# Scores of the first batch by pairs of heads, in two half-size PSUM areas, with a new step list

## The chip, the cores and the metric

One core of a Trainium2 chip runs the kernel. The core has five engines with queues of their own: TensorE (PE, matrix products; PEld is its loading of the stationary operand), VectorE (DVE), ScalarE (ACT), GpSimd (POOL) and SyncE (SP, which here only starts transfers). They wait for each other by semaphores. TensorE writes only to PSUM, which has eight banks of 512 fp32 columns on 128 partitions; ACT and DVE read it. Transfers (DMA) between main memory and the on-chip SBUF are started from the queues of SP, ACT and POOL and run beside the engines. The metric is the device time of one execution in microseconds (us), the median over several runs.

## The reference

The kernel computes attention with a forgetting gate for 8 batches of 8 heads, 576 positions and 64 features, and then a two-layer network on the result. Inputs and output are float32.

```python
scores = scale * np.matmul(q, k.transpose(0, 1, 3, 2))       # 8 x 8 x 576 x 576
cum = np.cumsum(np.log(np.clip(f, 0.0001, 1.0)), axis=-1)
scores = np.where(causal, -1e9, scores + cum[:, :, :, None] - cum[:, :, None, :])
attn = np.exp(scores - max); attn = attn / (sum(attn) + 1e-09)
x = np.matmul(attn, v)                                        # to 4608 x 512
h = x @ w_in                                                  # 512 x 2048
out = (h * sigmoid(h)) @ w_out                                # 2048 x 512
```

The part of the decay that depends on the query falls out of the quotient, so the kernel multiplies the values, and the ones of the denominator, by `exp(-cum)` of their key, and leaves the scores themselves alone.

## The kernel before

**Units of work.** A unit `n` is a batch and half its heads: `n = 2 * batch + group`, 16 units of four heads. Of each unit, q and k are loaded as four transfers each (L120), a strip of 32 partitions per head; they are cast to bf16 (L136 on POOL; one cast, the keys of n=0, on ACT, L134) and transposed in blocks of 32 by DVE (L279). After that a head's 64 features lie as two halves of 32 in its strip of 32 partitions. A score is therefore two matmuls of 32 rows each, accumulated (L350), with `tile_position` at the strip of the head. Keys stand on the PSUM partitions and queries along the columns. Only the key blocks at or below the diagonal are computed: 576 + 448 + 320 + 192 + 64 = 1600 columns a head.

**Scores.** `chunk` (L315) takes a score area `sc` of four banks, one bank of 512 columns per head (`patt`, tag `att`, one buffer), fills it, and has ACT write `exp(scale * sc)` as bf16 to `u` for all four heads in one instruction (L360). For batch 0 (n = 0 and 1) the 1600 columns are laid out so that queries 0 to 255 come first, then 256 to 511, then the rest, and are cut at 384, 832, 1280 and 1600 (`SPLIT_CUTS`, L307): steps `S n.c` (L367). There the causal mask is added by a matmul of an identity with a block of -30000 (`neg`, L338), ahead of the scores that it covers. For the other 14 units the columns of all units form one stream, cut every 512: steps `s0` to `s43` (L371). Their mask is applied to `u` afterwards by POOL (L387, steps `m`).

**Products.** `products` (L399) makes denominators and numerators from `u`: `w_bf` or the weighted values `vp` as stationary operand, four heads side by side on 32 output partitions each (L429). For batch 0 it uses one-bank areas `pn`: steps `f`, `h` (queries 0 to 255), `d`, `n` (256 to 511) and `e` (512 to 575), where f and d make a unit's denominators and h and n its numerators. The f's take log and exp of the denominator on ACT (L450, L451), the d's a reciprocal on DVE (L453). Whole units later use the same four-bank area as the scores (`ps`, steps `D`, `N`, `P`), with reciprocals in quarters (steps `R`, L468). DVE multiplies numerator and reciprocal into `xT` (L457).

**Network.** The first layer makes `hp` of 128 by 512 by four matmuls (L482), ACT takes tanh (L490) and DVE forms `gt` (L493): steps `A`. For the first group of 512 tokens it goes in halves of 256 tokens: 32 steps `H`. Steps `B` are quarters of an output tile of the second layer, four matmuls each (L516); every fourth `B` ends with a copy on ACT (L526) and a store (L527). `w_in` comes in four quarters, steps `I0` to `I3`, two transfers each from POOL's queue (L190); step `H` number 1 to 4 needs I0, 5 to 8 I1, 9 to 12 I2, 13 to 16 I3, and so again for the second 16. `w_out` comes in four steps `O`. Areas `pn`, `wps`, `hp`, `po` and the idle matmul's come from one pool of four one-bank buffers (`pbig`), in turn.

**Order.** Nothing is scheduled by a planner when the kernel is built. The text `ORDER` (L18) is a list of steps, and each engine's queue holds its instructions in the order of that list. Steps `y`, `z` are cast and transpose of the first 256 positions of n = 0 and 1; `G`, `c`, `t` loading, cast and transpose of their rest; `L`, `C`, `T` loading, cast and transpose of a later unit; the digit after the point is 0 for q and 1 for k. `l`, `u`, `w` are the log, the running sum and exp, and the transpose of the decay. `W b.c` loads a chunk of 128 values of a batch, `V b.c` multiplies it by the weights on POOL. `Z1` is one matmul on zeros whose result is not used. `g`, `o` are transfers of one element that wait for a quarter of a weight.

Of the kernel before, what the change touches and what calls it, by code (L numbers as in the profile page):

```python
# [12 lines left out]
P = 128  # L13
# [5 lines left out]
    l y0.0 y0.1 u z0.1 z0.0 w z1.1 y1.0 S0.0 G0.0 G0.1 z1.0 W0.3 V0.0 c0.0 c0.1 S1.0 I0 t0.0  # L19
    W0.2 t0.1 f0 V0.1 G1.1 S0.1 V0.3 I1 f1 G1.0 L2.1 V0.2 h0 c1.0 c1.1 W0.4 h1 L2.0 S0.2 I2  # L20
    d0 H H I3 S0.3 t1.0 t1.1 H C2.1 C2.0 S1.1 L3.0 n0 H H O2 T2.1 S1.2 H H d1 L3.1 H H S1.3
    n1 V0.4 H H H H H H T2.0 H O1 H C3.0 H H O0 L4.1 T3.0 s0 e0 L4.0 H H O3 s1 C3.1 H W1.4 H
    H T3.1 Z1 m2.0 s2 W1.3 H H H W1.0 g1 s3 e1 H m2.3 H s4 H m3.0 W1.1 H m2.1 m2.4 m3.1 m2.2
    H C4.1 B s5 m3.3 W1.2 B T4.1 m3.2 C4.0 B B D2 T4.0 R2.0 V1.4 B B R2.2 R2.3 B V1.3 s6
    V1.0 L5.0 L5.1 B m3.4 V1.1 W2.4 V1.2 C5.0 B C5.1 L6.0 C6.0 W2.2 B R2.1 P3 R3.1 B B W2.3
    R3.2 R3.0 B s7 B L6.1 m4.0 R3.3 B N3 g2 B W2.0 T5.0 T5.1 A g3 s8 A m4.2 L7.0 A A s9 T6.0
    V2.2 m4.1 m4.3 A m4.4 A A m5.0 D4 A A C6.1 V2.0 V2.3 s10 R4.2 L7.1 A A V2.4 T6.1 A m5.1
    s11 A W2.1 A A R4.3 s12 A B m5.3 W3.4 L8.1 B C7.0 m5.4 m6.0 V2.1 C7.1 V3.4 L8.0 R4.1 B
    s13 B B m5.2 m6.1 W3.2 R4.0 T7.0 T7.1 s14 B C8.0 W3.1 B C8.1 L10.1 W3.0 B P5 R5.1 V3.1
    R5.0 B m6.2 L9.1 B B W4.1 R5.3 s15 m6.4 B B T8.1 B o1 m6.3 R5.2 L9.0 V3.0 P6 W4.4 B V3.2  # L30
    T8.0 B m7.0 A A W3.3 s16 A V3.3 A A L10.0 W4.0 A R6.3 s17 A C10.1 A A C9.0 C10.0 A s18
    T9.0 A C9.1 A m8.0 A R6.2 s19 R6.1 A A V4.4 m7.4 A m7.2 B T9.1 m7.3 s20 B m7.1 B R6.0
    m8.2 V4.1 B P7 L12.0 B R7.3 m8.1 B B W5.4 W4.2 s21 m8.4 W5.1 R7.2 R7.0 W4.3 R7.1 L11.0 B
    B m8.3 B L11.1 T10.1 P8 B B A A s22 V4.3 R8.1 m9.0 A A B s23 B V5.4 T10.0 V4.2 A A R8.3
    s24 L12.1 A m9.3 C11.0 A A R8.2 s25 B A C11.1 A W5.2 s26 T11.1 V4.0 A A m9.1 B T11.0 s27
    m9.4 m9.2 m10.3 m10.2 R8.0 A A A B P9 R9.0 W5.3 C12.1 B R9.2 B m10.0 B s28 C12.0 R9.1 B
    B m10.4 m10.1 L13.0 T12.0 R9.3 V5.1 B C13.0 L14.0 L14.1 P10 B A V5.3 A R10.1 B L13.1 B
    W5.0 T12.1 V5.2 s29 A B R10.2 R10.3 B W6.2 A s30 A A m11.1 A m11.0 A C13.1 s31 m11.2 A B
    A m12.0 T13.0 T13.1 s32 V5.0 W6.1 R10.0 B m11.3 B A C14.1 L15.1 m12.1 s33 B A m11.4 A
    P11 A A m12.2 A R11.0 L15.0 R11.1 C15.1 B V6.1 s34 C15.0 W6.0 m12.4 m12.3 B B B R11.3  # L40
    V6.0 R11.2 P12 B A A A T14.1 s35 W6.4 B C14.0 V6.4 B W6.3 m13.0 B B s36 V6.3 W7.1 R12.3
    T14.0 m13.2 R12.2 A A V6.2 A B s37 A A R12.1 B s38 B W7.2 B A m14.0 m13.3 m13.4 s39
# [10 lines left out]
def kernel(  # L53
# [43 lines left out]
    patt = ctx.enter_context(tc.tile_pool(name="patt", bufs=1, space=bass.MemoryType.PSUM))  # L97
    pbig = ctx.enter_context(tc.tile_pool(name="pbig", bufs=4, space=bass.MemoryType.PSUM))

# [215 lines left out]
    def chunk(pieces):  # L315
        sc = patt.tile([P, QH, 512], FP32, name="sc", tag="att")
# [18 lines left out]
        for n, kb, q0, w, o, low in runs:  # L335
            if low:
                for j in range(QH):
                    nc.tensor.matmul(  # L338
                        sc[:, j, o : o + w],
                        lhsT=ident[:, :],  # L340
                        rhs=neg[:, P - w : P],
                        start=first,
                        stop=False,
                    )
                first = False
        for i, (n, kb, q0, w, o, low) in enumerate(runs):
            for x in range(2):
                for j in range(QH):
                    r = slice(j * 32, (j + 1) * 32)
                    nc.tensor.matmul(  # L350
                        sc[:, j, o : o + w],
# [7 lines left out]
        for n, c0, c1 in pieces:  # L359
            nc.scalar.activation(  # L360
                out=us[n][:, :, c0:c1],
                in_=sc[:, :, at : at + c1 - c0],
                func=ACT.Exp,
                scale=scale,
            )
            at += c1 - c0

    def scores(n, c):
        chunk([(n, SPLIT_CUTS[c], SPLIT_CUTS[c + 1])])


    def stream(i):
# [7 lines left out]
        chunk(pieces)  # L380
# [211 lines left out]
    for step in ORDER.split():  # L592
        if step == "H" and gpool is None:
            setup_pool.__exit__(None, None, None)
            gpool = ctx.enter_context(tc.tile_pool(name="gpool", bufs=2))
# [31 lines left out]
```

## Time and profile before

| what | value |
|---|---|
| median of 9 runs | 353.06 us (352.22 to 353.87) |
| the profiled execution | 353.87 us, span 352.1 us |
| PE busy | 327.5 us, 93% of the span |
| DVE, ACT, POOL busy | 223.3, 209.8, 128.9 us |
| moved by DMA | 42.54 MB, mean 121 GB/s |
| the chain that ended last, by engine | PE 79%, DMA 5%, ACT 4%, DVE 4%, SP's queue 3% |

The span goes from the first to the last instruction in the trace; what the run's time has on top lies around it. A line of the chain or of the order in time begins with the start and the duration in us. Then come engine, line of the kernel, operation and tiles, output ahead of the arrow and inputs behind it, with partitions and elements, and how many such instructions (x). The brackets at the end give how long the engine had been idle before, and whose end released it. In the tables of stretches, each stretch has its length, then for each engine the busy time and the number of instructions, then the granted PE clock, the mean busy share of the DMA engines and GB/s. Matmuls overlap and their ends are modelled, so the starts are the safer reading.

### The profile page before, as it was taken

The page shows a single profiled execution, that of the slowest core. Times are in us where ns is not written, and L with a number is a line of the kernel's source. Part 1 is how long each engine was busy: PE and PEld are TensorE (multiplying, and loading weights), DVE is VectorE, ACT ScalarE, POOL GpSimd, SP SyncE. Part 2 cuts the span into 40 slices and gives each one's busy share as a digit, 9 for nine tenths or more (in the row PEclk, how much of TensorE's full clock was granted, in tenths as well). Part 3 has the DMA queues.
Part 4 walks back from the last instruction along what each step waited for, and adds up shares of the span by engine and source line. Part 5 has one row for each costly group of instructions (what it writes and reads, how often), then busy time and mean ns, then how long its engine had stood idle before and what let it go on. Part 6 is the DMA issues. An engine that isn't in the chain of part 4 may idle for free.

```text
span 352.1 us, 8957 instructions
## 1 busy us (share of the span) xinstructions
PE 327.5 (93%) x3739; PEld 168.3 (48%) x3782; DVE 223.3 (63%) x297; ACT 209.8 (60%) x298; POOL 128.9 (37%) x172
## 2 busy tenths in 40 slices
PE   0677989999999999999999999999999999999996
PEld 0455765544455445543454455454545444444444
DVE  4457684788858786788868677679566844334210
ACT  3565698359953893499538855776574344444421
POOL 6763627818385182236453545222141000000000
PEclk9999899999999999999999999999999999999999
DMA  7999999898659803960298242223100000010102
GB/s 163 192 210 222 234 216 210 228 228 191 151 125 242 210 10 95 221 182 1 62 251 216 51 128 79 60 61 90 48 30 32 32 30 33 31 60 30 61 30 89
DMA packets 86416, 42.54 MB, mean 121 GB/s; under 512 B 41128, under 2 KB 81832, under 8 KB 86376
## 3 DMA queue, kind: packets, MB, share of 16 engines
q1 hardware_dynamic: 80936, 37.39, 42.8%
q0 software_dynamic: 4864, 4.33, 7.9%
q8 instruction: 29, 0.48, 0.6%
q10 hardware_dynamic: 576, 0.26, 0.3%
q14 instruction: 11, 0.09, 0.1%
HBM read 36.85 MB, written 9.44 MB: 131 GB/s over the span
## 4 chain that ended last, share of the span: by engine, by line
PE 79%; DMA 5%; ACT 4%; DVE 4%; SPq 3%; issue 3%; POOL 0%; ACTq 0%; POOLq 0%
PE po L516 34%; PE hp L482 30%; PE ps L429 9%; PE sc L350 6%; SPq L120 3%; DMA w_in_bf<-in_moe_w_in_dram 3%; DVE gt L493 2%; ACT u L360 2%; DMA stg<-in_q_dram 2%; ACT th L490 1%; DMA f_sb<-in_f_dram 1%; DVE xT L457 1%; SPq L144 1%; PE pn L429 0%; DVE qkT L279 0%
## 5 line engine op out<-in xcount | busy, mean ns | idle before, releaser
L493 DVE SCALAR_TENSOR_TENSOR gt<-th,hp 128x512 bf16<-128x512 bf16 (+1 forms) x160 | 96.4, 628 | 74.0 <-ACT th L490 73.2
L482 PE MATMUL hp<-xT,w_in_bf 128*128 128x512 bf16 (+1 forms) x622 | 137.0, 361 | 2.2 <-DMA w_in_bf<-in_moe_w_in_dram 1.3
L516 PE MATMUL po<-w_out_bf,gt 128*128 128x512 bf16 (+1 forms) x567 | 130.9, 373 | 3.1 <-issue 2.7
L360 ACT ACTIVATE u<-sc 128x2048 bf16<-128x2048 f32 (+7 forms) x64 | 95.0, 1503 | 21.9 <-PE sc L350 21.8
L490 ACT ACTIVATE th<-hp 128x512 bf16<-128x512 f32 (+1 forms) x160 | 84.0, 559 | 39.8 <-PE hp L482 36.7
L482 PEld LDWEIGHTS <-w_in_bf 128*128 128x128 bf16 x640 | 60.2, 99 | 64.8 <-issue 5.9
L516 PEld LDWEIGHTS <-gt 128*128 128x128 bf16 x592 | 55.4, 98 | 63.8 <-issue 2.8
L387 POOL TENSOR_SCALAR_AFFINE_SELECT u<-u 128x512 bf16<-128x512 bf16 (+1 forms) x70 | 40.0, 590 | 88.7 <-ACT u L360 88.3
L468 DVE RECIPROCAL rec<-rec 128x144 f32<-128x144 f32 x56 | 55.6, 1022 | 3.8 <-ACT rec L448 3.8
L279 DVE STREAM_TRANSPOSE qkT<-raw 128x1152 bf16<-128x1152 bf16 (+2 forms) x36 | 46.5, 1308 | 4.9 <-POOL raw L136 4.9
L263 POOL TENSOR_TENSOR vp<-vf,w_bf 128x512 bf16<-128x512 f32 (+1 forms) x40 | 41.4, 1041 | 18.4 <-DMA vf<-in_v_dram 17.5
L136 POOL CAST raw<-stg 128x1152 bf16<-128x1152 f32 (+2 forms) x34 | 36.0, 1072 | 28.6 <-DMA stg<-in_q_dram 25.0
L526 ACT ACTIVATE osb<-po 128x512 f32<-128x512 f32 (+1 forms) x37 | 21.7, 587 | 29.8 <-PE po L516 28.7
L350 PE MATMUL sc<-qkT 32*128 32x64 bf16 (+7 forms) x1064 | 33.6, 257 | 4.1 <-ACT u L360 3.3
L448 ACT ACTIVATE rec<-ps 128x192 f32<-128x192 f32 (+1 forms) x28 | 10.0, 408 | 43.4 <-DVE xT L457 43.1
L350 PEld LDWEIGHTS <-qkT 32*128 32x128 bf16 x1064 | 18.6, 99 | 24.8 <-issue 21.0
L457 DVE TENSOR_TENSOR xT<-ps,rec 128x512 bf16<-128x512 f32 (+1 forms) x28 | 19.9, 753 | 16.2 <-PE ps L429 16.1
L429 PEld LDWEIGHTS <-vp 128*32 128x32 bf16 x960 | 20.8, 100 | 4.5 <-issue 1.2
L429 PE MATMUL ps<-u,vp 128*32 128x320 bf16 (+4 forms) x784 | 21.6, 261 | 0.1
L429 PEld LDWEIGHTS <-w_bf 128*32 128x32 bf16 x480 | 9.2, 97 | 12.1 <-issue 8.4
L429 PE MATMUL ps<-u,w_bf 128*32 128x192 bf16 (+2 forms) x392 | 12.2, 263 | 0.1
L251 PE MATMUL wps<-ident_f,wexp 64*128 64x64 f32 x5 | 0.8, 316 | 8.0 <-ACT wexp L244 8.0
(37 smaller groups left out, 49.6 us busy)
## 6 DMA issues: line engine op xcount, KB each, us to landing
out_dram<-osb SPq DMA_DIRECT2D x35, 256.0 KB, 2.2
vf<-in_v_dram SPq DMA_DIRECT2D x32, 256.0 KB, 4.1
stg<-in_k_dram SPq DMA_DIRECT2D x56, 144.0 KB, 4.1
stg<-in_q_dram SPq DMA_DIRECT2D x56, 144.0 KB, 4.1
w_in_bf<-in_moe_w_in_dram POOLq DMA_DIRECT2D x8, 256.0 KB, 8.5
w_out_bf<-in_moe_w_out_dram POOLq DMA_DIRECT2D x4, 512.0 KB, 11.0
vf<-in_v_dram SPq DMA_DIRECT2D x8, 128.0 KB, 3.7
stg<-in_q_dram SPq DMA_DIRECT2D x8, 80.0 KB, 4.5
```

Source lines behind the costliest of these rows:

```text
L136: eng.tensor_copy(out=raw[n][:, i, r], in_=stg[n][:, i, r])
L263: nc.gpsimd.tensor_tensor(out=vp[r, c, :, :, :], in0=vst[b][c][r, :, :].rearrange("p h (r x) -> p h x r", x=2), in1=w_bf[r, c, b * H : (b ...
L279: nc.vector.transpose(out=qkT[n][g0 * R * T][:, i, :, :].rearrange("p x (g t c) -> p g c x t", t=T, c=R), in_=raw[n][:, i, g0 * E : g1 * E ...
L350: nc.tensor.matmul(sc[:, j, o : o + w], lhsT=qk_cols(n, r, 1, x, k_off(kb), P), rhs=qk_cols(n, r, 0, x, q0, w), start=(x == 0 and not unde ...
L360: nc.scalar.activation(out=us[n][:, :, c0:c1], in_=sc[:, :, at : at + c1 - c0], func=ACT.Exp, scale=scale,)
L387: nc.gpsimd.affine_select(out=x, in_=x, pattern=[[0, QH], [1, w]], compare_op=ALU.is_ge, fill=0.0, base=0 if kb < NM else ST, channel_mult ...
L429: nc.tensor.matmul(ps[32 * j : 32 * j + 32, o0 + q0 - e0 : o0 + q1 - e0], lhsT=w, rhs=us[n][:, j, o : o + q1 - q0], start=(kb == 0), stop= ...
L468: nc.vector.reciprocal(out=recs[n][:, r], in_=recs[n][:, r])
L482: nc.tensor.matmul(hp[:, 0 : hi - lo], lhsT=w_in_bf[:, cc, fc * P : (fc + 1) * P], rhs=xT[:, cc, t0 + lo : t0 + hi], start=(cc == 0), stop ...
L490: nc.scalar.activation(out=th[:, 0 : hi - lo], in_=hp[:, 0 : hi - lo], func=ACT.Tanh, scale=0.5)
L493: nc.vector.scalar_tensor_tensor(out=gt[:, fc, lo:hi], in0=th[:, 0 : hi - lo], scalar=1.0, in1=hp[:, 0 : hi - lo], op0=ALU.add, op1=ALU.mult,)
L516: nc.tensor.matmul(po[:, 0 : c1 - c0], lhsT=gt[:, fc, tb * P : (tb + 1) * P], rhs=w_out_bf[:, fc, c0:c1], start=(fc == 0), stop=(fc == NFC ...
```

## The change

The four-bank area `patt` is no longer made at the start. In its place stands a pool `psd` with two buffers of two banks each, which is closed ahead of step `s0`; `patt` is then made in the same four banks and serves as before. `chunk` is given a pool and a range of heads. A step `S n.c.x` of batch 0 makes the scores of heads 2x and 2x+1 only, in an area of `psd`, and one exp for these two heads. There are sixteen such steps in place of eight. Streams `s0` to `s43` are unchanged in content.

```diff
-    patt = ctx.enter_context(tc.tile_pool(name="patt", bufs=1, space=bass.MemoryType.PSUM))
     pbig = ctx.enter_context(tc.tile_pool(name="pbig", bufs=4, space=bass.MemoryType.PSUM))
+    psd_pool = tc.tile_pool(name="psd", bufs=2, space=bass.MemoryType.PSUM)
+    psd = psd_pool.__enter__()
+    patt = None
...
-    def chunk(pieces):
-        sc = patt.tile([P, QH, 512], FP32, name="sc", tag="att")
+    def chunk(pieces, pool, heads=range(QH)):
+        nh, h0 = len(heads), heads[0]
+        sc = pool.tile([P, nh, 512], FP32, name="sc", tag="att")
...
-                for j in range(QH):
+                for j in range(nh):
                     nc.tensor.matmul(
                         sc[:, j, o : o + w],
...
-                for j in range(QH):
+                for j in heads:
                     r = slice(j * 32, (j + 1) * 32)
                     nc.tensor.matmul(
-                        sc[:, j, o : o + w],
+                        sc[:, j - h0, o : o + w],
...
-                out=us[n][:, :, c0:c1],
+                out=us[n][:, h0 : h0 + nh, c0:c1],
...
-    def scores(n, c):
-        chunk([(n, SPLIT_CUTS[c], SPLIT_CUTS[c + 1])])
+    def scores(n, c, x):
+        chunk([(n, SPLIT_CUTS[c], SPLIT_CUTS[c + 1])], psd, range(2 * x, 2 * x + 2))
...
-        chunk(pieces)
+        chunk(pieces, patt)
...
     for step in ORDER.split():
+        if step == "s0":
+            psd_pool.__exit__(None, None, None)
+            patt = ctx.enter_context(
+                tc.tile_pool(name="patt", bufs=1, space=bass.MemoryType.PSUM)
+            )
```

The step list is new from end to end. Its steps are the same but for the scores of batch 0, one more `Z1`, and the one-element transfers (g1, g2, o1 left out, g0 and o3 added). Its beginning, before and after:

```diff
-    l y0.0 y0.1 u z0.1 z0.0 w z1.1 y1.0 S0.0 G0.0 G0.1 z1.0 W0.3 V0.0 c0.0 c0.1 S1.0 I0 t0.0
-    W0.2 t0.1 f0 V0.1 G1.1 S0.1 V0.3 I1 f1 G1.0 L2.1 V0.2 h0 c1.0 c1.1 W0.4 h1 L2.0 S0.2 I2
-    d0 H H I3 S0.3 t1.0 t1.1 H C2.1 C2.0 S1.1 L3.0 n0 H H O2 T2.1 S1.2 H H d1 L3.1 H H S1.3
-    n1 V0.4 H H H H H H T2.0 H O1 H C3.0 H H O0 L4.1 T3.0 s0 e0 L4.0 H H O3 s1 C3.1 H W1.4 H
-    H T3.1 Z1 m2.0 s2 W1.3 H H H W1.0 g1 s3 e1 H m2.3 H s4 H m3.0 W1.1 H m2.1 m2.4 m3.1 m2.2
+    y0.1 G0.0 l y0.0 u z0.1 y1.0 G0.1 c0.0 z0.0 W0.3 z1.0 S0.0.0 z1.1 t0.0 I0 S1.0.0 c0.1
+    G1.0 w S1.0.1 V0.0 t0.1 G1.1 S0.0.1 S0.1.1 c1.0 f1 W0.2 t1.0 S0.2.0 V0.1 S0.2.1 c1.1
+    L2.1 t1.1 I1 S0.3.0 Z1 L2.0 h1 L3.0 S0.1.0 S1.1.0 f0 S1.2.1 S0.3.1 d0 h0 S1.3.0 H H C2.1
+    W0.4 V0.2 I2 L3.1 H T2.1 H H C2.0 V0.3 S1.3.1 Z1 H L4.1 I3 S1.2.0 T2.0 S1.1.1 H H d1
+    C3.0 L4.0 n0 s0 H H H H O0 T3.0 O2 s1 n1 V0.4 H C3.1 H H H H H H H H H H T3.1 s2 W1.4 O1
+    m2.0 O3 m2.2 e0 H H s3 W1.0 m2.3 e1 H H H H m2.1 H s4 C4.1 H H m2.4 m3.0 W1.2 B s5 m3.2
```

In the old list the step after this piece is `H C4.1 B s5`; from `s5` on both lists hold the same matrix work, and all but a few of the same loads, casts and masks, in another order.

## The prediction

> **What bounds the kernel now.** I read first the busy time by stage, to see where TensorE (PE) is not full.
>
> ```profile
> core 0: us, PE busy (x) PEld busy (x) DVE busy (x) ACT busy (x) POOL busy (x), PEclk, DMA share, GB/s
> 8.00:28.00 20.00, 15.48 (x281) 10.68 (x285) 9.83 (x15) 11.74 (x14) 13.23 (x17) 1.00 1.05 207
> 28.00:38.00 10.00, 8.16 (x182) 5.82 (x171) 6.21 (x10) 6.06 (x9) 4.57 (x5) 0.83 1.21 229
> 38.00:56.40 18.40, 15.99 (x292) 11.45 (x295) 13.61 (x29) 16.23 (x28) 7.03 (x11) 1.00 1.21 217
> 56.40:334.90 278.50, 273.87 (x2924) 132.60 (x2966) 188.81 (x238) 169.32 (x239) 98.41 (x124) 1.00 0.42 107
> 334.90:352.10 17.20, 14.00 (x80) 7.69 (x79) 1.33 (x2) 3.16 (x6) 0.00 (x0) 1.00 0.17 61
> ```
>
> From 56.4 us on PE is busy 273.87 of 278.50, then ends with 14.00 of second-layer products and 3.2 of output. Only the first 56.4 us have slack: after the unavoidable first 8 us of loading, 4.5 + 1.8 + 2.4 = 8.8 us of idle PE. I therefore compare both kernels at one step, `s5`. Ahead of it both lists hold all of batch 0, `s0` to `s4`, all 32 `H` and one `B`; its scores start at 56.36 now. What follows is the same work, full on PE in either order. So the change is worth what `s5` moves, and some tenths.
>
> Next, PE in order of time within that head, with idle and releaser in brackets.
>
> ```profile
> 12.04 1.01 PE L338 MATMUL sc<-neg,ident 128*128 128x128 bf16 x8 [1.56 <-ACT u L360]
> 12.98 0.82 PE L350 MATMUL sc<-qkT 32*128 32x128 bf16 x24
> 15.36 0.94 PE L350 MATMUL sc<-qkT 32*128 32x256 bf16 x16 [1.11 <-ACT u L360]
> 16.52 1.50 PE L429 MATMUL pn<-u,vp 128*32 128x256 bf16 x32
> 21.70 0.72 PE L429 MATMUL pn<-u,w_bf 128*32 128x256 bf16 x12 [1.43 <-ACT u L360]
> 22.36 1.89 PE L482 MATMUL hp<-xT,w_in_bf 128*128 128x256 bf16 x8
> 28.43 1.05 PE L482 MATMUL hp<-xT,w_in_bf 128*128 128x256 bf16 x8
> 29.86 0.57 PE L350 MATMUL sc<-qkT 32*128 32x64 bf16 x32
> 34.69 0.61 PE L482 MATMUL hp<-xT,w_in_bf 128*128 128x256 bf16 x2 [1.27 <-DMA w_in_bf<-in_moe_w_in_dram]
> ```
>
> Two things are to be seen. PE waits for an exp (ACT L360) because the score area has one buffer of four banks: a score cannot be written until the exp before it has read. And the same eight `hp` matmuls take 1.89 us at 22.36 and 1.05 at 28.43: PE runs at half speed until about 28. (The clock column shows 1.00 there; I believe the durations.) It halves once more, at 34.70 to 38.10, where that column has 0.50, after the stretch with 1.27 and 0.57 of idle.
>
> Last, the exps on ACT and the two stretches of the chain of waits that are DMA:
>
> ```profile
> 13.86 1.45 ACT L360 ACTIVATE u<-sc 128x1536 bf16<-128x1536 f32 x1 [1.88 <-PE sc L350]
> 19.99 1.66 ACT L360 ACTIVATE u<-sc 128x1792 bf16<-128x1792 f32 x1 [1.25 <-PE sc L350]
> 36.21 1.24 ACT L360 ACTIVATE u<-sc 128x1280 bf16<-128x1280 f32 x1 [0.50 <-PE sc L350]
> 16.71 6.62 DMA stg<-in_q_dram
> 25.68 8.96 DMA w_in_bf<-in_moe_w_in_dram
> ```
>
> Loads and weights share DMA that is full (share 1.05 to 1.21): a weight quarter lands 6 to 11 us after POOL issues it.
>
> **Part 1, pairs cost PE time.** Before, 16 matmuls of four heads (8 of 256, 8 of 192 columns) took 0.94: two rounds of 256 and two of 192 at 1.2 columns/ns are 0.75, and about 0.19 to drain. 24 of 128 in 0.82 are six rounds, 0.64 + 0.18. So four heads, on four strips of 32 rows, run at once. A pair has only two strips: half the matmuls, the same number of rounds, the same time. The eight scores of batch 0 (0.82, 0.82, 0.94, 0.94, 0.72, 0.94, 0.57, 0.72 in the trace; 6.8 if all slow) become sixteen: +6.8 us of PE at half speed, +4.2 at full (0.57 against 0.94 is 0.61). No row has two strips alone; the bounds are 0 (if a strip's rounds could run twice as fast, which nothing shows) and these. I take these. The skill's page TensorE: Matmul & The Clock Gate, section Part 3: Packing small matmuls, gives 3.07x for four row tiles, not 4: two at a perfect 2x would then cost only 1.5 times, +3.4 slow. The rows fit whole rounds of four, so I keep +6.8.
>
> **Part 2, ACT.** From 1280 to 1792 columns 0.42 us, so 0.82 ns a column and 0.19 fixed. Sixteen exps of 768, 896, 896 and 640 are 4 x (0.82 + 0.92 + 0.92 + 0.71) = 13.5 against 12.0: +1.5 us, on an ACT that is busy 11.74 of 20 there. That lies in idle time until about 22, and on the path behind it.
>
> **Part 3, what is removed.** With two areas PE fills one while ACT reads the other: the 1.56, 1.11, 1.43, 0.37 and 0.57 us waits for an exp go, 5.0 us; and a continuous PE should reach full speed earlier. The 1.27 wait for weights may go or grow (part 5).
>
> **Part 4, the walk.** By the new order, with these durations. The key half of n=0 is cast on ACT ahead of the log; with its transpose (0.69) and that of the query half, S0.0.0 is at 8.6 to 9.4. Query n=1 is cast at 9.1 to 9.7 as now and both n=1 transposes end at 11.1: S1.0.0 to 11.95, the wexp transposes (0.76) to 12.7, S1.0.1 to 14.0, S0.0.1 to 15.3. S0.1.1 waits for t0.1, whose cast stands behind I0 (1.49 on POOL), until 16.1. From there PE has no gap: S0.1.1, f1, S0.2.0, S0.2.1 and S0.3.0 end at 21.2 slow, h1 about 22. Before, four whole scores, f0, f1, h0, h1 and d0 are done by then; here four scores' worth, f1, h1. PE is some 2 us behind.
>
> Then speed matters. From 22.5 ACT is the chain: its exps end at 23.5, 24.4, (log and exp of f0) 25.2, 26.1, 26.8, 27.5, the table load (1.28) at 28.8. At full speed PE keeps up: d0 at 25.4, its reciprocal (1.76) to 27.1, product to 27.8, first `H` 27.8. Slow: 30.1.
> When does it get fast? Now PE was full from 16.0 to 20.27 without it, and it came at about 28 after 24.4 to 27.8. The same page, Part 1: The HAM clock gate, says 3.4 us of sustained work suffices, in free-running windows of that length: that is 19.5 at the earliest here; by the trace, which needed a window with nearly no idle, 19.5 to 22.9, mean 21.2. By the page's shortest I would gain nothing further, since ACT bounds.
> With 27.8: H1 to H4 fill the four one-bank areas; H5 waits for gt of H1 and weight quarter I1, 30.0; remaining scores end at 33.1, d1 34.7, n0 35.7, s0 36.3. H11 and H12 wait for d1's reciprocal and n0's product (37.3, 38.0), s1 at 39.0, n1 40.2, H13 to H23 45.8 (ACT th and DVE gt 0.42 each set the pace after s1's exp), s2, e0, H24 to H25 to 48.3, s3, e1, H26 to H30 to 52.2, s4, H31, H32, B, and `s5` at 54.7. Gain: 56.36 - 54.7 = 1.7 us. The extra `Z1` (0.22 to 0.4) is inside.
>
> **Part 5, moved loads.** POOL has I1 behind c1.1 instead of ahead of it. SP has v chunk 2 (256 KB) behind n=1, so those loads come 1.2 us earlier and, without I1 beside them, perhaps 2: c1.1 to 21.7, I1 issued to 23.2 (now 19.1), L2.1 cast by 24.4, V0.2, I2 to 26.9 (now 26.4), L2.0 cast, V0.3, I3 to 30.5 (now 27.9). With 6 to 9 us: I1 29 to 30, I2 34 to 35.5, I3 39 to 40.5. Needed: H5 30.0, H9 36.3, H13 40.2. All hidden, by about nothing for I1 and I3. Each later us is a us at `s5`. On SP the chunk 4 load moves behind two stg loads, needed only by e0 at 46; L4 waits for a stg buffer, as now. The gates g1, g2, o1 go and g0, o3 come, 0.7 us of issue each on SP, ahead of outputs that have slack. w_out is issued from 32 (now 35.6), needed at 54: hidden, with up to 15 us to land.
>
> **Part 6, the later order.** 4.6 us of idle in 278 can move either way: -0.7 to +0.7, taken as 0.
>
> Sum: -1.7. The profiled run is 353.87 with span 352.1; it would be 352.2. Its own time is 0.8 over the median shown, 353.06; on the median I forecast 351.4.
>
> **Rivals.** (a) *PE stays slow to the end of the scores.* It speaks for it that two strips may not count as full activity, and that 4.3 us did not suffice at 16. First `H` 30.1, 2.3 later, partly caught up where ACT waited: `s5` at 57 to 58.5, +1.4: 354.5. It is slower from a full-speed start later than about 26.
> (b) *Weights late.* I3 is three POOL steps later than now; if L2.1 lands at 28.6 as now, rather than 23, I2 is issued to 31.1 and I3 to 36, landing at 39.5 and 44: H13 waits 3.5 us, less 0.5: +1.5, 354.5. It decides from a landing of L2.1 beyond 25. Against: without I1 to I3 beside it, it has less to share with.
> (c) *The gain is larger:* the 2.3 us of score waits at 43 to 54 vanish since more `H` lie between streams: `s5` 52.7, -3.6: 349.5.
> (d) *Nothing:* doubled PE time and removed waits cancel, 353.06.
>
> **How the numbers follow.** Likeliest, -1.7 with its own 350.4 to 352.2: 0.44. (a) 0.17, (b) 0.13, (c) 0.13, (d) 0.13. Range 348.8 to 355.2: from (c) less part 6, to (a) or (b) with 0.7 from each of part 6 and the other. Measurement tells 0.2%, 0.7 us. Faster: 0.44 + 0.13 = 0.57; same 0.13; slower 0.30.
>
> **What would show it.** Scores of one pair as long as those of four heads (0.8 to 0.95 slow, 0.5 to 0.65 fast). No idle of PE for ACT L360 over 0.5 from 16 to 26. `hp` x8 near 1.05 from its first group, starting near 28. POOL's fourth weight issue by 23.5, eighth by 31. First `H` later than 22.36 by 5 to 6 us, yet `s5` ahead of 56.36. Wrong: pairs taking half the time; slow `hp`; a PE wait for w_in of over 1 us; or equal `s5` and another end.

## The result, and the profile after

The changed kernel takes 356.66 us (median of 17 runs, 354.79 to 357.56); the kernel before took 353.06 beside it. The ratio is 1.0094, with a 95% interval of 1.0078 to 1.011: slower by 3.3 us (the two medians differ by 3.6), where 1.7 us of gain were forecast. The profiled execution of the changed kernel took 357.41 us, its span is 355.7.

The same stages as before the change, with the third cut at the start of `s5`'s scores (59.40 us; it was 56.36):

```profile
core 0: us, PE busy (x) PEld busy (x) DVE busy (x) ACT busy (x) POOL busy (x), PEclk, DMA share, GB/s
8.00:28.00 20.00, 15.22 (x215) 10.35 (x218) 7.07 (x11) 10.79 (x16) 8.25 (x12) 1.00 0.96 195
28.00:38.00 10.00, 9.10 (x153) 6.80 (x148) 6.24 (x10) 6.84 (x12) 9.81 (x12) 1.00 1.21 225
38.00:59.40 21.40, 19.31 (x377) 13.84 (x375) 17.16 (x34) 18.28 (x33) 7.97 (x11) 1.00 1.18 215
59.40:338.50 279.10, 273.84 (x2922) 132.72 (x2965) 189.48 (x238) 170.57 (x239) 96.79 (x122) 1.00 0.44 105
338.50:355.70 17.20, 13.81 (x80) 7.64 (x78) 0.51 (x1) 3.16 (x6) 0.00 (x0) 0.99 0.20 76
```

From `s5` to the end it is 296.3 us, against 295.8 before. So 3.04 us of the loss between the two profiles lie ahead of `s5` and about 0.5 behind it.

What TensorE waited for between 9 us and `s5` (engine, tile and line, the releaser, us in total, times, longest):

```profile
PE sc L354 <- DVE qkT L282: 6.9, 2, 6.3
PE pn L435 <- POOL vp L266: 2.5, 1, 2.5
PE hp L488 <- DVE xT L463: 1.5, 2, 0.9
PE pn L435 <- ACT u L364: 0.4, 1, 0.4
PE sc L354 <- ACT u L364: 0.4, 1, 0.4
```

The 6.9 us of the first row are nearly all the wait for the first loads, and two more rows of 0.5 and 0.3 us are left out here. Before the change the rows for ACT's `u` were 3.3, 2.0 and 1.6 us; now they are 0.8 together. The waits that the change was to remove are gone, and the kernel is slower.

TensorE in order of time, in the rows that answer to those shown of before:

```profile
9.21 0.82 PE L354 MATMUL sc<-qkT 32*128 32x128 bf16 x12 [6.30 <-DVE qkT L282]
20.62 0.40 PE L435 MATMUL pn<-u,vp 128*32 128x256 bf16 x4 [0.47 <-issue]
23.52 0.62 PE L435 MATMUL pn<-u,vp 128*32 128x128 bf16 x12 [2.50 <-POOL vp L266]
26.66 0.93 PE L354 MATMUL sc<-qkT 32*128 32x64 bf16 x16
28.39 0.94 PE L435 MATMUL pn<-u,w_bf 128*32 128x256 bf16 x16
31.73 3.65 PE L488 MATMUL hp<-xT,w_in_bf 128*128 128x256 bf16 x20 [0.91 <-DVE xT L463]
40.40 0.61 PE L354 MATMUL sc<-qkT 32*128 32x512 bf16 x8
40.94 2.07 PE L488 MATMUL hp<-xT,w_in_bf 128*128 128x256 bf16 x16
```

Three things are to be seen. A pair's scores take as long as four heads' (0.82 and 0.93 us). The first `H` stands at 31.73, not at 22.36 as before. And its 20 matmuls take 3.65 us where 16 take 2.07 at 40.94: TensorE ran at half speed until about 34.

### The profile page after: what moved, and what is told of

It is laid out like the page before. It is cut to its first block, busy times and chain, and to the rows that moved or that the text cites. A ratio compares the mean times of both kernels' runs of the same rounds, so it can differ in the third digit from the quotient of the medians.

```text
span 355.7 us, 8959 instructions
## 1 busy us (share of the span) xinstructions
PE 331.9 (93%) x3737; PEld 171.8 (48%) x3783; DVE 223.1 (63%) x297; ACT 212.2 (60%) x306; POOL 128.1 (36%) x172
## 4 chain that ended last, share of the span: by engine, by line
PE 75%; issue 7%; DMA 6%; POOL 4%; SPq 4%; ACT 3%; DVE 0%; ACTq 0%; POOLq 0%
PE hp L488 31%; PE po L522 30%; PE ps L435 8%; PE sc L354 5%; DMA stg<-in_k_dram 4%; SPq L123 3%; ACT u L364 2%; DMA stg<-in_q_dram 2%; POOL vp L266 1%; POOL u L393 1%; POOL raw L139 1%; ACT osb L532 1%; SPq L147 1%; DVE xT L463 0%; POOL w_out_bf L202 0%
## 5 line engine op out<-in xcount | busy, mean ns | idle before, releaser
L364 ACT ACTIVATE u<-sc 128x2048 bf16<-128x2048 f32 (+9 forms) x72 | 96.0, 1357 | 24.2 <-PE sc L354 24.0
L496 ACT ACTIVATE th<-hp 128x512 bf16<-128x512 f32 (+1 forms) x160 | 84.9, 559 | 36.2 <-PE hp L488 34.2
L488 PEld LDWEIGHTS <-w_in_bf 128*128 128x128 bf16 x640 | 61.0, 99 | 64.9 <-issue 6.0
L474 DVE RECIPROCAL rec<-rec 128x144 f32<-128x144 f32 x56 | 54.8, 1019 | 3.9 <-ACT rec L454 3.9
L354 PE MATMUL sc<-qkT 32*128 32x128 bf16 (+7 forms) x1064 | 38.9, 256 | 7.8 <-DVE qkT L282 6.9
L532 ACT ACTIVATE osb<-po 128x512 f32<-128x512 f32 (+1 forms) x37 | 21.7, 587 | 30.5 <-PE po L522 30.5
L354 PEld LDWEIGHTS <-qkT 32*128 32x128 bf16 x1064 | 22.3, 99 | 29.0 <-issue 19.7
L454 ACT ACTIVATE rec<-ps 128x192 f32<-128x192 f32 (+1 forms) x28 | 10.0, 408 | 44.2 <-DVE xT L463 43.0
L342 PE MATMUL sc<-neg,ident 128*128 128x128 bf16 (+1 forms) x40 | 5.7, 282 | 2.3 <-POOL neg L170 2.3
```

The lines of the kernel that those rows point to most:

```text
L354: nc.tensor.matmul(sc[:, j - h0, o : o + w], lhsT=qk_cols(n, r, 1, x, k_off(kb), P), rhs=qk_cols(n, r, 0, x, q0, w), start=(x == 0 and not ...
L364: nc.scalar.activation(out=us[n][:, h0 : h0 + nh, c0:c1], in_=sc[:, :, at : at + c1 - c0], func=ACT.Exp, scale=scale,)
L474: nc.vector.reciprocal(out=recs[n][:, r], in_=recs[n][:, r])
L488: nc.tensor.matmul(hp[:, 0 : hi - lo], lhsT=w_in_bf[:, cc, fc * P : (fc + 1) * P], rhs=xT[:, cc, t0 + lo : t0 + hi], start=(cc == 0), stop ...
L496: nc.scalar.activation(out=th[:, 0 : hi - lo], in_=hp[:, 0 : hi - lo], func=ACT.Tanh, scale=0.5)
```

## Where the loss can be read: s0

The row at 40.40 above is `s0`, the first stream step. In the old list 19 of the 32 `H` stand ahead of `s0`, in the new one only 8, so 11 `H` and `n1` moved behind it. In the profiles of all runs the stretch behind it is nearly constant: `s0` to `s5` takes 13.4 us in the old list (14.0 in one run), 18.9 to 19.1 in the new one. It is longer only where the profile lists one more wait in it: by 0.5 us in e14, for weights, and by 1.2 to 1.9 in e5, e9 and e10 (below). From `s5` to the end it is 295.8 in the old list and 296.3 in the new. With 1.7 us around the span, a run of the new list takes `s0` + 19.0 + 296.3 + 1.7, which is `s0` + 317.0. To match a kernel before of 352.5, the level that it has beside most of the experiments, `s0` has to start at 35.5. The changed kernel's median answers to 39.7; in its profile `s0` is at 40.40. The experiments ask why `s0` is that late.

The table gives the median, the ratio to the kernel before measured beside it with its 95% interval, and from each run's one profile: when TensorE reached full speed, the first `H`, `s0` and `s5`. The speed is from the clock changes that the trace records; ahead of the first of them the profile's clock column shows 1.00, but matmuls take twice their time. "Half" names a return to half speed. A profile shows one execution only, and loads don't land at the same time in each: one cast that waits for its load began at 21.76 us in one profile of the changed kernel and at 18.77 in the other. The expectations below call `s5` "batch 5's scores" and `s0` "batch 0's first stream step"; the steps are meant.

| run | median us | ratio | full speed from | first H | s0 | s5 |
|---|---|---|---|---|---|---|
| before | 353.06 | | 27.8, half 34.7 to 38.1 | 22.36 | 42.97 | 56.36 |
| changed | 356.66 | 1.0094 [1.0078, 1.0110] | 34.4 | 31.73 | 40.40 | 59.40 |
| e8_again (changed, once more) | 355.70 | 1.0087 [1.0059, 1.0115] | 32.6 | 28.76 | 37.98 | 56.98 |
| e2_pairs_old_list | 352.68 | 0.9998 [0.9978, 1.0019] | 25.2, half 28.6 to 32.1 | 22.37 | 43.64 | 57.66 |
| e3_fours_new_list | 358.44 | 1.0152 [1.0119, 1.0185] | 34.6, half 38.0 to 41.5 | 28.82 | 42.48 | 61.42 |
| e1_v_first | 355.74 | 1.0076 [1.0049, 1.0103] | 31.5 | 28.83 | 37.45 | 56.45 |
| e4_fill | 354.96 | 1.0063 [1.0039, 1.0087] | 23.1 | 28.78 | 36.72 | 55.83 |
| e5_full_speed | 359.94 | 1.0185 [1.0137, 1.0233] | 4.7 | 28.07 | 38.38 | 59.25 |
| e9_light_fill | 359.27 | 1.0186 [1.0162, 1.0210] | 6.7, half 20.4 to 34.0 | 31.58 | 40.33 | 60.54 |
| e10_v_first_light_fill | 357.93 | 1.0144 [1.0119, 1.0170] | 5.6, half 15.8 to 32.9 | 29.46 | 38.68 | 59.00 |
| e7_full_speed_old | 352.37 | 1.0012 [0.9991, 1.0033] | 4.0 | 21.00 | 40.31 | 53.70 |
| e11_pairs_old_fast | 353.36 | 1.0024 [1.0004, 1.0045] | 6.4, half 16.6 to 30.3 | 21.91 | 42.92 | 56.32 |
| e6_early_h | 358.32 | 1.0153 [1.0123, 1.0182] | 34.4 | 25.16 | 40.09 | 59.09 |
| e12_half_scores_new | 355.36 | 1.0065 [1.0041, 1.0089] | 34.4 | 28.49 | 38.43 | 57.44 |
| e13_half_scores_old | 353.17 | 1.0008 [0.9989, 1.0028] | 25.2, half 28.6 to 32.0 | 21.92 | 42.68 | 56.07 |
| e14_half_scores_v_first | 355.41 | 1.0068 [1.0044, 1.0092] | 32.2 | 28.12 | 37.31 | 56.80 |
| e15_f0_h0_ahead | 355.59 | 1.0067 [1.0042, 1.0092] | 32.4 | 24.57 | 37.80 | 56.81 |
| e16_ahead_v_first_fill | 355.61 | 1.0066 [1.0045, 1.0086] | 25.0 | 26.54 | 38.61 | 57.61 |
| e17_ahead_half_scores | 354.79 | 1.0053 [1.0035, 1.0072] | 38.6 | 23.82 | 39.44 | 58.44 |
| e18_weights_ahead | 356.80 | 1.0135 [1.0109, 1.0162] | 24.4, half 31.3 to 38.1 | 26.21 | 39.80 | 58.80 |

## Pairs or list

```diff
# e2_pairs_old_list: the changed code, with the old list
-    ... z1.1 y1.0 S0.0 G0.0 ... c0.1 S1.0 I0 ...
+    ... z1.1 y1.0 S0.0.0 S0.0.1 G0.0 ... c0.1 S1.0.0 S1.0.1 I0 ...
# e3_fours_new_list: the code of before, with the new list, four heads at the later pair's place
-    ... S0.0.0 z1.1 t0.0 I0 S1.0.0 c0.1 G1.0 w S1.0.1 V0.0 t0.1 G1.1 S0.0.1 ...
+    ... z1.1 t0.0 I0 c0.1 G1.0 w S1.0 V0.0 t0.1 G1.1 S0.0 ...
```

> The pairs alone: the list of the kernel before, in which each score step is replaced by its two pairs one behind the other; areas as in the changed kernel. My theory (the order is to blame, the pairs are about neutral): the pairs add 4 to 7 us of PE time and 1.5 of ACT in the head and take away up to 5 us of waits for an exp, so 352.5 to 355 (0.998 to 1.005). Rival 1 (the doubled PE time is the loss): 356 or more (1.008 and above).

> The new list alone: scores of four heads in the one four-bank area as before, each at the place of the later of its two pairs. My theory: the wait of PE for V0.1 stays (h1 at 23.5), the waits for exps come back, PE has 4 us less work and no more speed: first network matmul 30 to 32, 355.5 to 357.5 (1.007 to 1.013). Rival 1: without the doubled PE time the loss is gone, 351.5 to 353.5 (0.996 to 1.001).

Pairs in the old list change nothing (0.9998). The new list with four heads at a time costs 1.5%, more than either forecast. So the list is the loss, and pairs win back some 0.6% within it (1.0152 against 1.0094). That the pairs cost TensorE time is true all the same: up to `s5` it is busy 39.6 us before, 43.8 in the profile of e2, while its idle time falls from 16.8 to 13.9.

## One wait on GpSimd, and half speed

The new list puts V0.1, which batch 0's second numerators need, on GpSimd's queue behind the cast of column c1.0, and that waits for loads. In the changed kernel's profile:

```profile
21.76 0.72 POOL L139 CAST raw<-stg 128x640 bf16<-128x640 f32 x1 [5.35 <-DMA vf<-in_v_dram]
22.43 1.04 POOL L266 TENSOR_TENSOR vp<-vf,w_bf 128x512 bf16<-128x512 f32 x1
```

TensorE stood 2.5 us for V0.1. The cast's row names the value load `vf` as the last to land. In the second profile of the same kernel the cast was at 18.77 and TensorE did not wait for V0.1.

```diff
# e1_v_first
-    ... S1.0.1 V0.0 t0.1 ... t1.0 S0.2.0 V0.1 S0.2.1 c1.1
+    ... S1.0.1 V0.0 V0.1 t0.1 ... t1.0 S0.2.0 S0.2.1 c1.1
# e4_fill: five more matmuls on zeros
-    ... S0.3.0 Z1 L2.0 h1 ...
+    ... S0.3.0 Z6 L2.0 h1 ...
```

> The changed kernel with one step moved in its list: the weighting of value chunk 1 (V0.1, 1.04 us on POOL) stands right behind V0.0 instead of behind the cast c1.0. My theory: in the changed kernel V0.1 waits on POOL behind a cast whose data land at 21.7 us, PE waits 3.0 us for it at 20.2 to 23.5 in step h1, and this gap also keeps PE at half speed until 34.4. Then h1 runs at 20.6 here, PE is full from 14 to about 22, the first network matmul comes near 28.5 instead of 31.7, s5 near 56.5 instead of 59.4, the time is about 353.7 (ratio to the kernel before 1.002). Rival 1, the doubled PE time of the pairs is the loss and the gap only hides part of it: 355.7 to 357 (1.008 to 1.011). Rival 2, other moved loads (weights I1 to I3) are the loss: no change, 356.7.

> The changed kernel with six matmuls on zeros instead of one in the idle step ahead of h1: 2.2 us more of PE work whose result is not used, put into the 3.0 us gap, to keep PE busy while it waits for V0.1. It tells the gap itself from the speed that it costs. My theory: PE is full from 14 to 23, reaches full speed at 20 to 24 instead of 34.4, the first network matmul comes at 29 to 30.5 instead of 31.7, the time is 354.5 to 355.5 (1.004 to 1.007). If the speed has nothing to do with the gap: 356.7 to 357.2 (1.010 to 1.012).

> The changed kernel once more, for a second profile and for its time beside the other three. All theories: 356.3, ratio 1.009. If the 2.5 us wait of batch 0's second numerator for GpSimd in the first profile came from a late landing of column c1.0, the wait is about 1 us when the piece lands near 19.5 us; the first `H` stands near 29 to 32 either way.

e1's interval overlaps that of the changed kernel: a late c1.0 explains the one profile, not the median. e4 came as its theory had it, but the step is small: 0.24% under e8 with intervals of that size. Its profile shows what six full matmuls did, beside e8 (the second profile of the changed kernel) without them. First e8:

```profile
24.76 0.71 PE L354 MATMUL sc<-qkT 32*128 32x64 bf16 x20
27.14 0.71 PE L354 MATMUL sc<-qkT 32*128 32x64 bf16 x20
28.76 4.21 PE L488 MATMUL hp<-xT,w_in_bf 128*128 128x256 bf16 x20 [0.90 <-DVE xT L463]
37.98 0.61 PE L354 MATMUL sc<-qkT 32*128 32x512 bf16 x8
```

Then e4:

```profile
19.27 2.74 PE L217 MATMUL idle<-zero 128*128 128x512 bf16 x6
25.41 0.46 PE L354 MATMUL sc<-qkT 32*128 32x64 bf16 x20
28.78 2.13 PE L488 MATMUL hp<-xT,w_in_bf 128*128 128x256 bf16 x18 [1.40 <-DVE xT L463]
36.72 0.61 PE L354 MATMUL sc<-qkT 32*128 32x512 bf16 x8
```

The scores at 25 us are at full speed in e4 and at half in e8. The first `H` doesn't move by that (28.78 and 28.76): both wait for `xT`. The 20 `hp` matmuls then take 4.21 us in e8 and 2.13 and 0.39 in e4 with a short wait for weights between, and `s0` is 1.3 earlier. The price of that speed is inside: `h1`, at 20.14 in e8, starts at 21.94 behind the five more matmuls.

Does full speed from the start bring more? These five add unused matmuls on zeros: many, many in the old list, few, few with V0.1 first, and few with pairs in the old list.

```diff
+    Z24 y0.1 G0.0 l ...          # e5, e7 (e7: ahead of the old list); Z22 in e9, e10, e11
+            for _ in range(2):   # at the head of each score of batch 0; e9 to e11: one, for x = 0 only
+                nc.tensor.matmul(sc[:, 0, :], lhsT=zero[:, 0:P], rhs=zero[:, :], start=True, stop=True)
```

> The changed kernel with extra unused work added: 24 matmuls on zeros as the first step, and two more at the head of each pair chunk of batch 0's scores (written into the score area before that chunk's own results). The array is then active over all its rows from the first microseconds. Theory (the loss is half-speed time, because scores in two of four strips don't bring full speed and the first full-array `H` now starts 6 to 9 us later than in the kernel before): full speed from before 10 us on, first `H` at 26 to 28, batch 5's scores at 55 to 56.5, median 352.5 to 354, ratio 1.000 to 1.004. Rival (the speed isn't the cause; the order of the work and the waits for loads are): batch 5's scores at 58.5 or later, 357 or more.

> The kernel before (four heads at a time, its own list) with the same unused work on zeros added: 24 matmuls as the first step and two at the head of each chunk of batch 0's scores. Theory (half-speed time costs wherever TensorE sets the pace): full speed some 18 us earlier than 27.8, median 351 to 352, ratio 0.994 to 0.998; the gain is less than in the changed kernel, since its `H` is earlier. Rival (speed isn't the limit of this stretch, the loads and casts are): 353, ratio 1.000.

> The changed kernel with little extra unused work: 22 matmuls on zeros as the first step, while TensorE waits for loads anyway, and one more ahead of the first pair chunk of each score of batch 0 (8 in all, 0.22 us each at full speed, 1.8 us), so that full speed comes early without the 7 us on the path that the heavier filling cost. TensorE was busy 44 to 45 us ahead of batch 5's scores in the changed kernel, some 8 us of it for half speed. Theory (TensorE bounds the changed head of the kernel, and half speed until the first window of full-array `H` is what makes it too long): full speed from about 5 us on and held, first `H` at 26 to 27.5, batch 5's scores at 54 to 56, median 352 to 354, ratio 0.999 to 1.005. Rival (speed buys nothing, as it bought nothing in the kernel before: casts, exps and loads set the pace): 355.5 to 357, ratio 1.008 to 1.013.

> As the light filling of the changed kernel (22 matmuls on zeros first, one ahead of each score of batch 0), and V0.1 right behind V0.0, so that batch 0's second numerators don't stand behind the cast of column c1.0. Theory: full speed and no wait of TensorE for GpSimd ahead of them; 0.3 us or so less than without the move: 351.7 to 353.5, ratio 0.998 to 1.003. Rival (speed buys nothing): 355.5, ratio 1.0075, as with the move alone.

> The changed kernel's code with the list of the kernel before (each score split into its two pairs), and the light filling (22 matmuls on zeros first, one ahead of each score of batch 0). Pairs in the old list took as long as the kernel before, with 4 us more of busy TensorE at half speed against removed waits. Theory (pairs cost TensorE time, which full speed gives back, and remove waits for exps): 350.5 to 352, ratio 0.993 to 0.999. Rival (exps, casts and loads set the pace there): 352.6, ratio 1.000.

The theory missed in all five; in the old list the rival was right, and speed buys nothing that the medians show (1.0012, 1.0024). In the new list the filled kernels are slower than the changed one, but they don't tell what speed without a price would be worth. From 9 us to `s0` TensorE is busy 24.94 us in e5 and 26.84 in e8. About 7 us of e5's are filling (32 matmuls of 0.22), so half speed costs some 9 us there, as an estimate from these two, and the filling used up most of it. In e9 and e10 the speed was lost again long before the first `H`. And e5, e9 and e10 have a wait of their own behind `s0`, which made it 20.2 to 20.9 us to `s5`. It is released by nothing that the profile shows; in e9:

```profile
53.96 1.70 PE L493 MATMUL hp<-xT,w_in_bf 128*128 128x256 bf16 x14
57.19 0.82 PE L493 MATMUL hp<-xT,w_in_bf 128*128 128x256 bf16 x6 [1.54 <-issue]
```

It is 2.18 us in e5, 1.64 in e10, and absent in all other runs. Its cause stays open.

## Is it TensorE's time at all

```diff
# e12_half_scores_new, e13_half_scores_old, and e14 with V0.1 first
             for x in range(2):
+                v = 1 if n < QB and x == 1 else w
...
-                        sc[:, j - h0, o : o + w],
+                        sc[:, j - h0, o : o + v],
```

> The changed kernel with half of batch 0's score work left out: of the two matmuls that make a score, the second covers one column instead of all, so the number of instructions and their order stay. A pair chunk's matmuls then take about half: 0.82 to 0.93 us to some 0.45 at half speed, over sixteen chunks up to 6 us. Theory (the changed head of the kernel is bound by busy TensorE, and the pairs' doubled score time is what fills it): batch 5's scores at 52 to 54.5, median 351 to 353, ratio 0.996 to 1.003, a gain of 4 to 5 on the changed kernel. Rival (its list's order of loads, casts and exps sets the pace): 355.5 to 356.5, ratio 1.009.

> The same cut in the kernel before (the second matmul of each score of batch 0 covers one column): eight scores of 0.94 us become 0.5, 3.2 us at most. There a score, its exp and the next score follow each other through one area, so what is left out shortens the chain. Theory: a gain of 1 to 3, 350 to 352, ratio 0.991 to 0.997, less than in the changed kernel. Rival (loads and casts set the pace): 352.6, ratio 1.000.

> The cut of the scores in the changed kernel, and V0.1 right behind V0.0, so that the second numerators of batch 0 don't stand behind the cast of column c1.0. With shorter scores TensorE reaches those numerators sooner, so GpSimd's delay shows more. Theory: 1 us less than with the cut alone, 350 to 352. Rival (GpSimd is hidden then too): as with the cut alone, within 0.3 us.

The gain of 4 to 5 us did not come. Half of the score work left out gives the changed kernel about 0.2% and the kernel before nothing. The profile of e12 shows where it went:

```profile
20.63 0.62 PE L436 MATMUL pn<-u,vp 128*32 128x128 bf16 x12 [1.42 <-POOL vp L266]
23.95 0.56 PE L355 MATMUL sc<-qkT 32*128 32x128 bf16 x12 [0.41 <-DVE qkT L282]
28.49 4.43 PE L489 MATMUL hp<-xT,w_in_bf 128*128 128x256 bf16 x20 [1.05 <-DVE xT L464]
33.84 0.89 PE L489 MATMUL hp<-xT,w_in_bf 128*128 128x256 bf16 x4
38.43 0.61 PE L355 MATMUL sc<-qkT 32*128 32x512 bf16 x8
```

TensorE, with less to do, waits for V0.1, for the transposes of n=1 and for `xT`. The first `H` is again at 28.5. And half speed lasts to 34.4, as in one profile of the changed kernel (32.6 in the other): `hp` x4 is still 0.89 at 33.84, where it is 0.60 at full speed.

## Chains ahead of s0

In most runs of the new list the first `H` is at 28 to 29.5. Ahead of it the list has column c1.1 (load, cast, transpose `t1.1`), `S1.1.0`, `f0`, `d0` with its reciprocal on DVE, and only then `h0`, whose product the first `H` needs.

```diff
# e6_early_h
-    ... S0.1.1 c1.0 f1 W0.2 ... L2.0 h1 L3.0 S0.1.0 S1.1.0 f0 S1.2.1 S0.3.1 d0 h0 S1.3.0 H H C2.1
+    ... S0.1.1 c1.0 f1 f0 W0.2 ... L2.0 h1 h0 H H L3.0 S0.1.0 S1.1.0 S1.2.1 S0.3.1 d0 S1.3.0 C2.1
# e15_f0_h0_ahead
-    c1.1 L2.1 t1.1 I1 S0.3.0 Z1 L2.0 h1 L3.0 S0.1.0 S1.1.0 f0 S1.2.1 S0.3.1 d0 h0 S1.3.0 H H C2.1
+    c1.1 L2.1 I1 S0.3.0 Z1 L2.0 h1 L3.0 S0.1.0 f0 h0 t1.1 S1.1.0 H H S1.2.1 S0.3.1 d0 S1.3.0 C2.1
# e16_ahead_v_first_fill: e15 with V0.1 right behind V0.0, and Z6 for Z1
# e17_ahead_half_scores: e15 with the halved scores
# e18_weights_ahead: e16 with
-    V0.1 t0.1 ... c1.1 L2.1 I1 S0.3.0 ... h0 t1.1 S1.1.0 H H S1.2.1 ... L3.1 H T2.1 H H C2.0
+    V0.1 I1 t0.1 ... c1.1 L2.1 S0.3.0 ... h0 H H H H t1.1 S1.1.0 S1.2.1 ... L3.1 T2.1 H C2.0
```

> The changed kernel with f0 moved behind f1, h0 behind h1 and the first two `H` behind h0: the full-array work starts earlier, the pairs and the rest of the list stay. Theory (half-speed time until full-array work): first `H` at 23 to 24, full speed at 27 to 28 as in the kernel before, median 353 to 354.5. Rival (the place of `H` doesn't matter): 356 to 357, ratio 1.009.

> The changed kernel with f0, h0 ahead of the transpose t1.1 and of S1.1.0, the first two H behind S1.1.0, d0 behind S0.3.1. In the changed list the first `H` stood behind the chain: key column c1.1 lands, GpSimd casts it, DVE transposes it, S1.1.0, f0, reciprocal of d0 on DVE, product of h0. Theory (this chain holds the first `H` at 28 to 29, whatever TensorE's load): products of h0 no longer wait for c1.1, first `H` at 24 to 25.5; the first four `H` come early, the later ones keep their places behind the scores; batch 0's first stream step s0 1 to 2 us earlier, median 354 to 355.5, ratio 1.003 to 1.007. Rival (TensorE's own order of work and speed hold the following steps): first `H` earlier, median unchanged, 356 to 357, ratio 1.009 or more.

> The same order with V0.1 right behind V0.0 and six matmuls on zeros instead of one ahead of h1, so full speed comes early. Theory: the gains of the three add in part (V0.1 0.7, filling 1.0): 352.5 to 354, ratio 1.000 to 1.004. Rival: they share one slack, 355, ratio 1.007.

> The same order, with the second matmul of each score of batch 0 cut to one column (half of the score work left out). In the changed list this cut alone gave 0.9 us. Theory (the chain behind c1.1 hid the cut; with h0 ahead of it TensorE's time counts): 2 to 3 us less than the order alone, 351.5 to 353, ratio 0.998 to 1.002. Rival (loads and casts hold it elsewhere too): within 1 us of the order alone.

> The last list (h0 ahead, V0.1 first, six matmuls on zeros ahead of h1) and, further, weight quarter I1 issued by GpSimd right behind V0.1, ahead of column c1.1 as in the kernel before, and the first four `H` right behind h0, ahead of t1.1. The step s0 then waits for none of: the products of h0 behind c1.1, a late I1 (TensorE waited 1.1 to 2.0 us for it once h0 was ahead), half speed in the later `H`. Theory (three near-equal chains end within 1 us of each other, so that taking away one or two gave no more than 0.9 us; with all three gone s0 moves): s0 at 35.5 to 37, batch 5's scores 19 us later as in every run of the new list, median 352.5 to 354, ratio 0.999 to 1.004. Rival (the transfers are full: I1 earlier makes c1.1 and what follows later by as much): s0 at 37.5 to 39, 355 to 356.5, ratio 1.006 to 1.010.

In e6 the first `H` came at 25.16, after 3.17 us of waiting for `xT`, because on DVE that product stood behind `t1.1`. Its eight matmuls did not bring full speed, which came at 34.4 as without them, and the kernel got slower. e15 took the chain away: first `H` 24.57, 4 us earlier than in e8, but `s0` at 37.80 against 37.98. Its ratio lies in its theory's range, but not for the theory's reason. TensorE itself was full there: it worked 27.35 of the 28.80 us from 9 us to `s0`, most of them at half speed. e16, which also has V0.1 first and full speed from 25.0, and e17 show what stands there next:

```profile
29.98 1.27 PE L488 MATMUL hp<-xT,w_in_bf 128*128 128x256 bf16 x10
33.21 0.39 PE L488 MATMUL hp<-xT,w_in_bf 128*128 128x256 bf16 x2 [1.97 <-DMA w_in_bf<-in_moe_w_in_dram]
38.61 0.61 PE L354 MATMUL sc<-qkT 32*128 32x512 bf16 x8
```

That is e16: the fifth `H` waits for weight quarter I1, which the new list issues behind c1.1 (at 24.31 on GpSimd, 17.64 in the kernel before). In e17 the same wait is 1.09 us, and half speed lasted to 38.6, over nearly the whole stretch. e18 issues I1 at 16.61. The wait for it is gone, and the kernel is slower again:

```profile
26.21 1.91 PE L488 MATMUL hp<-xT,w_in_bf 128*128 128x256 bf16 x16 [1.51 <-DVE xT L463]
29.86 0.51 PE L354 MATMUL sc<-qkT 32*128 32x128 bf16 x12 [0.76 <-DVE qkT L282]
32.26 1.03 PE L488 MATMUL hp<-xT,w_in_bf 128*128 128x256 bf16 x4
39.80 0.61 PE L354 MATMUL sc<-qkT 32*128 32x512 bf16 x8
```

The four early `H` put their `gt` on DVE ahead of `t1.1`, so `t1.1` ran at 28.91, though c1.1 was cast by 22.94. And speed fell to half once more from 31.3 to 38.1 (`hp` x4 1.03 us, against 0.60). The time lies beyond even the rival's range, and the rival's cause did not show: the cast of c1.1 began at 22.22, only 0.7 us after e8's (21.49).

So the cause is settled to this depth: the list, which puts 11 `H` and `n1` behind `s0` and doesn't bring `s0` forward by as much. The runs show no single chain that holds `s0`: taking away GpSimd's order, half of the scores, the chain through c1.1, or part of the half speed each left the ratio at 1.0063 to 1.0076, two or three together at 1.0053 to 1.0068, and three (c1.1, V0.1, speed) with I1 early at 1.0135.

One sum narrows the rest. These are the stretches from 9 us to `s0` in e8, e12, e15 and e16, with the columns of the first table: TensorE's busy time stands behind the comma.

```profile
9.00:37.98 28.98, 26.84 (x410) 18.73 (x410) 14.38 (x23) 18.53 (x29) 17.84 (x23) 1.00 1.15 211
9.00:38.43 29.43, 24.54 (x411) 17.10 (x412) 14.01 (x22) 18.47 (x29) 18.33 (x22) 1.00 1.13 214
9.00:37.80 28.80, 27.35 (x411) 18.59 (x411) 14.26 (x23) 18.53 (x29) 18.03 (x22) 1.00 1.06 202
9.00:38.61 29.61, 25.77 (x416) 17.22 (x415) 14.64 (x23) 18.17 (x29) 18.02 (x23) 1.00 1.05 198
```

For `s0` at 35.5 the stretch may last 26.5 us. In e8 and e15 TensorE's work alone is longer than that, so without less work or more speed no wait taken away would be enough. In e12 and e16 the work is shorter, but the idle time has grown from 2.1 us to 4.9 and 3.8. No run has both little work and little idle time. Whether one would bring `s0` early enough, and which chain would hold it next, stays open. No variant of the new list beat the kernel before, and none of the old list did.

## Why the prediction was wrong

The sum of the profiled run was 352.2 and it took 357.41, a miss of 5.2 us: 4.1 at `s0` (36.3 forecast, 40.40 measured), 0.6 from `s0` to `s5` (18.4 forecast, 19.0), about 0.5 behind `s5`. The step that failed is the walk to `s0` in part 4: it took full speed to come at 21.2 us, and it came at 34.4 and 32.6.

- **Part 1, pairs cost TensorE time: right.** 0.82 us for 12 matmuls and 0.93 for 16, as for 24 and 32; busy time ahead of `s5` rose from 39.6 to 44.2 us (45.0 in e8), within the +4.2 to +6.8. The smaller price, 1.5 times, set a perfect 2x for two strips beside the page's 3.07x for four; the trace has twice the time for a score. But e13 and e12 show that half of the score work, left out by itself, was worth next to nothing: other waits took its place.
- **Part 2, ACT: right.** Busy ahead of `s5` 37.24 before, 38.44 after: +1.2 for +1.5.
- **Part 3, removed waits: right.** 6.9 us of waits for `u` became 0.8. They were not a gain: the old list won nothing with the waits gone and the pairs' time added (e2), and nothing when half of the score work was left out (e13).
- **Part 4, the walk: failed here.** "From there PE has no gap" missed V0.1 behind c1.0: 2.5 us in one profile, none in the other. "Mean 21.2" for full speed was 32.6 and 34.4. In e8, without that late landing, `d0` is at 25.41 as forecast and the first `H` at 28.76 for 27.8; the half speed that I priced ahead of the first `H` (30.1) fell behind it instead, on the 20 `hp` matmuls, 4.21 us. `s0` was then 37.98, 1.7 late. The walk counted no such loss: from 9 us to its `s0` at 36.3 are 27.3 us, and in e8 TensorE's work alone took 26.84 of them. The prediction's own sign of being wrong, slow `hp`, is what came. Nor did 3.4 us of sustained work suffice for full speed (see the last section).
- **Part 5, moved loads: wrong in size, hidden at first.** I1 was issued by 26.1 (23.6 in e8) for 23.2, I2 by 31.5 for 26.9, I3 by 35.1 for 30.5: each POOL step waits for a load, as in

```profile
27.99 1.15 POOL L139 CAST raw<-stg 128x1152 bf16<-128x1152 f32 x1 [1.92 <-DMA stg<-in_k_dram]
30.09 1.45 POOL L193 DMA_DIRECT2D w_in_bf<-in_moe_w_in_dram  x2
```

  where L2.1 was to be cast by 24.4. TensorE waited at most 0.2 us for these weights in the changed kernel, since it was later itself; in e16 and e17 I1 became the wait.
- **Part 6:** about +0.5, inside the 0.7.
- **Rival (a), slow to the end of the scores**, happened: full speed came at 32.6 to 34.4, later than its limit of 26. Its price, 354.5, was too small. Whether it is the whole is not shown: with full speed at 23.1 (e4) 0.6% stays, with the time that the filling took inside. **Rival (b)**: its sign came, L2.1 was cast at 27.99 and 26.47, but not its wait. **(c)** fell; **(d)** describes e2, pairs in the old list.

With the measured lengths behind it, even `s0` at the forecast 36.3 gives 353.3 us: no gain. The larger part of the miss is the walk to `s0`. It took one landing time for each load and one time for full speed, all of them earlier than what came, and every later step moved with them.

## What to carry to other kernels

When a list moves work from ahead of a step to behind it, fix the length of what lies behind (here 19.0 against 13.4 us) and ask how much earlier the step must start to pay; then look for everything that could hold that start: each queue, each landing, and the engine's own work at the speed that it will have there. Removing a wait pays only as far as the next of these lets it (e15). Change one thing at a time: the area in pairs was harmless, the new order that came with it was not. Compare by medians: two profiles of the changed kernel differ by 2.4 us in `s5`.

## What the hardware showed

**A full TensorE can stay at half speed.** In e10 speed was lost at 15.8 us; from 15.87 to 28.98 TensorE then worked without a gap on scores on two strips, products, masks and single matmuls on zeros, and stayed at half. Five stretches of 3.41 us lie between the two recorded changes of its speed (busy time behind the comma, the clock third from the end):

```profile
15.80:19.21 3.41, 3.34 (x55) 2.39 (x55) 0.01 (x1) 2.05 (x3) 1.07 (x2) 0.50 1.09 198
19.21:22.63 3.42, 3.42 (x37) 1.24 (x33) 0.89 (x1) 1.21 (x2) 0.72 (x1) 0.50 1.13 228
22.63:26.04 3.41, 3.41 (x58) 2.19 (x58) 1.45 (x2) 2.69 (x5) 2.11 (x3) 0.50 1.07 220
26.04:29.46 3.42, 2.95 (x61) 1.92 (x56) 2.30 (x2) 1.32 (x3) 2.42 (x3) 0.50 1.05 168
29.46:32.87 3.41, 3.40 (x17) 2.35 (x17) 0.99 (x3) 2.64 (x5) 2.95 (x4) 0.50 1.16 244
29.46 3.99 PE L493 MATMUL hp<-xT,w_in_bf 128*128 128x256 bf16 x20 [0.48 <-DVE xT L468]
```

Full speed came only behind the fifth, which held nothing but `hp`, on all 128 rows; in e4 six full matmuls on zeros brought it. Which property of the work counts, its rows, its columns or the size of the matmuls, no run here separates. The Trainium skill's page TensorE: Matmul & The Clock Gate, section Part 1: The HAM clock gate, asks for some 3.4 us of sustained work; 13 us of these scores and products were not enough here, so the measurement decides. The recorded changes are whole multiples of 3.41 us apart, which agrees with the window of that length that the page gives. **Less work can be slower work:** with h0 ahead, full speed came at 32.4 with whole scores (e15) and at 38.6 with halved ones (e17), in one profile each.
